# An attention and experts kernel: three tiles for w1, raw tiles of their own for each kind of weights, eight result tiles

## The chip, the cores and the metric

One core of one Trainium2 chip runs the whole program. Times are device microseconds (us) of one execution. The kernel before took 694.74 us as the median of 3 runs (694.33 to 696.3).

## What is computed

Three stages follow each other: attention by random features, a gated block, and four experts whose outputs are mixed by weights. N = 1152 tokens (batch 2 x 576), D = 512 features, F = 1024. All of it is float32.

```python
q_p, k_p = phi(q * scale), phi(k * scale)     # phi: exp of a projection by omega
x = (q_p @ (k_p^T v)) / (q_p @ sum(k_p))      # heads joined: 1152 x 512
x = ((x @ w1) * (x @ w2)) @ w3 @ w_out        # the gated block
p = domain_probs / (domain_probs.sum(-1, keepdims=True) + 1e-09)
for e in range(4):
    out += p[:, e:e + 1] * (np.maximum(x @ ew1[e], 0.0) @ ew2[e])
```

## The kernel before

**Numbers as pairs.** A float32 operand of a matmul is held as a pair: a rounded high part and the rest (HI, LO). `split` makes one: ScalarE (ACT) writes the high part (L79), VectorE (DVE) subtracts it (L80). Three matmuls then stand for one product (`PASSES`). In the profile, "w1e<-raw" on ACT and "w1e<-raw,w1e" on DVE are the two halves of such a split.

**The stages.** Attention runs in pairs of heads, with parts of the gated block beside it. The product of w3 and w_out is folded into `w3o` (eight tiles of 4 KB in each partition). `gated` (L158) multiplies by w1 and w2, whose pairs lie in the pool `w1` (eight tiles of 4 KB). `expert_input` (L204) multiplies by the folded weights, first for batch 0, then for batch 1, eight groups of 24 matmuls each, and splits the experts' inputs, `x2`.

**The experts** run in eight half experts, two for each of the four. A half loads its weights (`load_w1`, `load_w2`), computes the hidden values (`hidden`, L690 on TensorE, PE) for two halves of the columns, forms sums of them (`sums`, tiles hs and hq), and multiplies by the second weights (`second`, L772, and `tails`, L799). Both products are done by Strassen's scheme with seven products in place of eight, so the weights are needed in sums and differences. `load_w1` loads two raw tiles of 4 KB, splits one (a w1e tile of 8 KB), splits a quarter (w1f, 4 KB), adds and subtracts raw parts in place (`place`, L586 on DVE, four times), splits the other raw tile (a second w1e tile), adds again and splits the first one once more (the third w1e tile). `load_w2` does much the same with two raw tiles and four w2e tiles. A product of `hidden` comes in groups of six matmuls: X1 Y1 X5 Y5 and so on in `ORDER`.

**The results.** `second` collects a token tile of results in an `o` tile. In the first seven halves GpSimd's queue adds it to the output in memory (`add_to`, L724). In the last half the output so far is read back into the nine `o` tiles (`results`, L734 on SyncE's queue, SP), DVE adds the last products (L749), and SP stores them (`store`, L740).

**What sets the order.** Each engine runs its instructions in one fixed order. A scheduler writes these orders when the kernel is built, from the dependences, the order of the code, and the tiles that are free: a pool with `bufs` tiles makes the next `tile()` wait until an earlier one has been read for the last time. Pools are placed in SBUF from its left and its right end like two stacks, so a pool that is opened after another was closed lies over the same bytes, and its tiles wait for the last reader there. On the right end the pools of the experts start where `w1` and `w3o` lay: first the pool of w1e and w1f, then w2e, and further in hid, hs, s and o. The raw tiles are a pool on the left.

```python
raw_p = ctx.enter_context(tc.tile_pool(name="raw", bufs=3, reuse_waits="tile"))
w1e_p, w2_p, hid_p, hs_p, s_p, o_p = right("w1e", 4), right("w2e", 4), right("hid", 1), ...
```

Of the kernel before, what the change touches and what calls it, by code (L numbers as in the profile page):

```python
# [8 lines left out]
F32 = mybir.dt.float32  # L9
# [6 lines left out]

HI, LO = 0, 1
HS_BUFS = 4
O_BUFS = 6
HALVES = 5  # L20


# [22 lines left out]
def attention_moe_kernel(ctx: ExitStack, tc: tile.TileContext, q, k, v, omega, mw1, mw2, mw3, mwo, probs, ew1, ew2, out):  # L45
# [6 lines left out]
    P = 128  # L52
# [82 lines left out]
    w12, hid, wo, w3o, x2, xf = {}, {}, [], [], {}, {}  # L135
# [108 lines left out]
    with ExitStack() as actx:  # L244
# [78 lines left out]
        for j in range(2):  # L323
            s = slice(j * D, (j + 1) * D)
# [27 lines left out]
        class Pair:  # L352
# [81 lines left out]
            def place(self):  # L434
                ps = bank("et")
                for r in range(R):
                    transpose(ps[:, r * P:(r + 1) * P], self.xs[:, r].rearrange("p j d -> p (j d)"))
                x, s = xt[self.b][self.i], MAIN_COLS
                split(x[:, HI, s], x[:, LO, s], ps)
# [100 lines left out]
                    else:  # L540
                        gated(at, 2, int(s[1]), int(s[2]), ("w", "po") * 2)

    raw_p = ctx.enter_context(tc.tile_pool(name="raw", bufs=3, reuse_waits="tile"))
    h_p = mctx.enter_context(tc.tile_pool(name="h", bufs=2 * KF + 2 * KD - XT_BUFS, reuse_waits="tile"))
    a_p = cctx.enter_context(tc.tile_pool(name="a", bufs=1, reuse_waits="tile", side="right"))
    for s in AFTER.split():
# [23 lines left out]
    GH = KE // 4  # L570
# [3 lines left out]
    def right(name, bufs):  # L574
        return ctx.enter_context(tc.tile_pool(name=name, bufs=bufs, side="right", reuse_waits="tile"))

    w1e_p, w2_p, hid_p, hs_p, s_p, o_p = right("w1e", 4), right("w2e", 4), right("hid", 1), right("hs", HS_BUFS), right("s", 2), right("o", O_BUFS)
    hd = hid_p.tile([P, 2 * GH, B, S], F32, name="hd")
    turn = [0]

# [7 lines left out]
    def parts(t, src):  # L588
        split(t[:, HI], t[:, LO], src)
        return t  # L590

    def combine(low, high, x11, x12, x21, x22, first, both):


        t = {}
        a = both(low)
        t["A11"], t["A12"] = a[0], a[1]
        t["A22"] = first(x22)
        place(x22, x21, x22, ALU.add)
        place(x21, x11, x21, ALU.subtract)  # L600
        a = both(high)
        t["S3"], t["S1"] = a[0], a[1]
        place(x11, x22, x11, ALU.subtract)
        place(x12, x12, x11, ALU.subtract)
        a = both(low)
        t["S2"], t["S4"] = a[0], a[1]
        return t

    def raw_half(src):
        r = raw_p.tile([P, 2, 512], F32, tag="raw", name="raw")  # L610
        nc.sync.dma_start(out=r.rearrange("p a (k f) -> p (a k) f", f=src.shape[2]), in_=src)
        return r

    def load_w1(hf):

        r = []
        for m in range(2):
            f0 = m * (EFF // 2) + hf * GH * P
            r.append(raw_half(ew1[e, :, f0:f0 + GH * P].rearrange("(k p) f -> p k f", p=P)))

        def both(src):
            t = parts(w1e_p.tile([P, 2, 2, 512], F32R, tag="w1e", name="w1e"), src)
            return [t[:, :, k].rearrange("p a (k f) -> p a k f", k=2) for k in range(2)]

        def first(src):
            t = parts(w1e_p.tile([P, 2, 512], F32R, tag="w1f", name="w1f", bufs=1), src)
            return t.rearrange("p a (k f) -> p a k f", k=2)

        return combine(r[0], r[1], r[0][:, 0], r[0][:, 1], r[1][:, 0], r[1][:, 1], first, both)

    def load_w2(hf):

        r = []
        for m in range(2):
            f0 = m * (EFF // 2) + hf * GH * P
            r.append(raw_half(ew2[e, f0:f0 + GH * P].rearrange("(g p) d -> p g d", p=P)))
        b = {(m, n): r[m][:, :, n * HD:(n + 1) * HD] for m in range(2) for n in range(2)}

        def both(src):
            return parts(w2_p.tile([P, 2, GH, DM], F32R, tag="w2e", name="w2e"), src)  # L640

        t = {}

        def named(x, one, two):
            t[one], t[two] = x[:, :, :, :HD], x[:, :, :, HD:]

        t["both"] = both(r[0]), both(r[1])
        named(t["both"][0], "B11", "B12")
        named(t["both"][1], "B21", "B22")
        place(b[0, 0], b[0, 1], b[0, 0], ALU.subtract)  # L650
        place(b[0, 1], b[1, 1], b[0, 1], ALU.subtract)
        named(both(r[0]), "T1", "T3")
        place(b[1, 1], b[1, 1], b[0, 0], ALU.subtract)
        place(b[1, 0], b[1, 0], b[1, 1], ALU.subtract)
        named(both(r[1]), "T4", "T2")
        return t
# [153 lines left out]
    for e in range(NE):  # L810
        for hf in range(2):
            fresh, last = e == 0 and hf == 0, e == NE - 1 and hf == 1
            with ExitStack() as order:
                for ins in (*pairs[-1].mark, pairs[-1].loaded):
                    order.enter_context(tc.issue_after(ins))
                w1t = load_w1(hf)
            hidden(w1t, 0)
            t0 = sums(0)
            w2t = load_w2(hf)
            hidden(w1t, 1)  # L820
            second(w2t, t0, 0, fresh, last)
            t1 = sums(1)
            tails(w2t, fresh, last)
            second(w2t, t1, 1, fresh, last)
# [30 lines left out]
```

## Time and profile before

| what | value |
|---|---|
| median of 3 runs | 694.74 us |
| the profiled execution: time, span | 693.17 us, 691.4 us |
| PE busy | 665.8 us, 96% |
| DVE busy | 482.7 us, 70% |
| ACT busy | 402.9 us, 58% |
| POOL busy | 163.8 us, 24% |
| mean granted clock of PE | 0.997 of full speed |

The span is the time from the first instruction to the last one; 1.77 us of the execution lie around it. PE's share is the largest by far, and matmuls overlap a little, so its busy time is no measure of its peak. The attention and the gated block end at about 259 us, `expert_input` at about 310 us; the rest is the experts. "DMA" in a table by stretches is the mean busy share of the 16 DMA engines.

### The profile page before, as it was taken

Reading aid. Unit: us, or ns where it says so; the run is one execution under the profiler, and the core shown is the slowest. Engines: PE = TensorE matmul, PEld = TensorE weight load, DVE = VectorE, ACT = ScalarE, POOL = GpSimd, SP = SyncE. Lnnn points to the kernel's source line nnn. Section 1 sums busy time; section 2 is a strip of 40 time slices with the busy share of each in tenths; the row PEclk is TensorE's granted clock in tenths of the full one; section 3 lists DMA queues with packets and bytes.
Section 4 is the critical chain, followed back from the end, with each engine's and each line's share of the span. In section 5 each row is a group of like instructions: output and inputs, shape, how many; then the busy total and the mean of one; then the engine's idle time right before and its main releaser. Section 6 shows DMA issues by size and latency. Waiting matters only on the chain.

```text
span 691.4 us, 12448 instructions
## 1 busy us (share of the span) xinstructions
PE 665.8 (96%) x4889; PEld 634.7 (92%) x4889; DVE 482.7 (70%) x782; ACT 402.9 (58%) x867; POOL 163.8 (24%) x155
## 2 busy tenths in 40 slices
PE   7898999999999999998999999999999999999997
PEld 6786778899999999998989999999999999999996
DVE  4888646669593222258987869877888688688795
ACT  5895445565452222246866676677676676686640
POOL 2865223259271000000021122230320311202200
PEclk9999999999999999999999999999999999999999
DMA  9764323235330000001143166372660762745715
GB/s 260 262 210 140 94 91 116 77 113 153 123 92 1 1 1 1 1 1 61 62 137 122 17 122 122 44 150 68 122 137 2 138 123 27 140 93 100 146 32 167
DMA packets 47146, 66.91 MB, mean 97 GB/s; under 512 B 7600, under 2 KB 30128, under 8 KB 47088
## 3 DMA queue, kind: packets, MB, share of 16 engines
q1 hardware_dynamic: 37792, 49.05, 22.8%
q0 software_dynamic: 8608, 16.52, 15.9%
q8 instruction: 38, 0.62, 0.4%
q10 hardware_dynamic: 688, 0.56, 0.3%
q14 instruction: 20, 0.16, 0.1%
HBM read 47.24 MB, written 18.87 MB: 96 GB/s over the span
## 4 chain that ended last, share of the span: by engine, by line
PE 73%; DVE 11%; DMA 6%; ACT 5%; issue 3%; POOL 1%; DVEq 0%; ACTq 0%; POOLq 0%; SPq 0%
PE ps_po L185 5%; PE ps_f L690 5%; PE ps_f L772 4%; DMA raw<-in_moe_w_dram 3%; PE ps_w L158 3%; PE ps_w L690 3%; PE ps_f L158 3%; PE ps_po L158 3%; PE ps_x L690 3%; PE ps_et L690 3%; PE ps_kv L690 2%; PE ps_t L690 2%; PE ps_po L690 2%; PE ps_kv L772 2%; PE ps_kv L412 2%
## 5 line engine op out<-in xcount | busy, mean ns | idle before, releaser
L724 POOL DMA_DIRECT2D out_dram<-o x70 | 57.7, 892 | 382.5 <-DVE o L749 206.6
L93 POOL TENSOR_SCALAR f64e<-f 128x512 f32<-128x512 f32 x40 | 66.8, 1673 | 78.1 <-DVE w3f L95 32.2
L80 DVE TENSOR_TENSOR hs<-hd,hs 128x1024 fp32r<-128x1024 f32 x48 | 58.4, 1219 | 3.1 <-ACT hs L79 2.4
L79 ACT ACTIVATE hs<-hd 128x1024 fp32r<-128x1024 f32 x48 | 50.7, 1056 | 7.9 <-DVE hd L586 4.9
L185 PE MATMUL ps_po<-wo,w3T 128*128 128x512 f32 x192 | 48.4, 400 | 3.3 <-DVE w3T L80 2.8
L690 PE MATMUL ps_f<-x,w1e 128*128 128x288 f32 x288 | 48.2, 298 | 3.1 <-DVE w1e L80 3.1
L674 ACT ACTIVATE hd<-hd 128x288 f32<-128x288 f32 x96 | 41.3, 439 | 15.6 <-DVE hd L672 14.9
L586 DVE TENSOR_TENSOR raw<-raw 128x512 f32<-128x512 f32 x64 | 43.9, 686 | 8.4 <-DMA raw<-in_moe_w_dram 8.1
L185 PEld LDWEIGHTS ps_po<-wo,w3T 128*128 128x128 f32 x192 | 34.8, 188 | 12.2 <-DVE w3T L80 3.9
L690 PEld LDWEIGHTS ps_f<-x,w1e 128*128 128x128 f32 x288 | 41.8, 191 | 3.7 <-DVE w1e L80 3.6
L94 DVE SCALAR_TENSOR_TENSOR f64e<-f,f64e 128x512 uint32<-128x512 uint32 x40 | 40.1, 1012 | 6.1 <-POOL f64e L93 5.8
L586 DVE TENSOR_TENSOR hd<-hd 128x512 f32<-128x512 f32 x64 | 43.9, 685 | 0.6
L79 ACT ACTIVATE w2e<-raw 128x1024 fp32r<-128x1024 f32 x32 | 33.5, 1058 | 17.7 <-PE ps_f L772 4.7
L772 PE MATMUL ps_f<-w2e,hs 128*128 128x256 f32 x288 | 42.6, 283 | 1.0 <-ACT o L746 0.6
L80 DVE TENSOR_TENSOR w2e<-raw,w2e 128x1024 fp32r<-128x1024 f32 x32 | 38.9, 1219 | 4.6 <-ACT w2e L79 4.5
L80 DVE TENSOR_TENSOR w1e<-raw,w1e 128x1024 fp32r<-128x1024 f32 x24 | 29.3, 1222 | 17.5 <-ACT w1e L79 17.2
L772 PEld LDWEIGHTS ps_f<-w2e,hs 128*128 128x128 f32 x288 | 38.1, 191 | 1.5 <-ACT o L746 0.8
L158 PE MATMUL ps_w<-xt,w 128*128 128x288 f32 x144 | 34.4, 298 | 0.0
L79 ACT ACTIVATE w1e<-raw 128x1024 fp32r<-128x1024 f32 x24 | 25.4, 1059 | 15.2 <-DMA raw<-in_moe_w_dram 10.3
L158 PE MATMUL ps_po<-xt,w 128*128 128x288 f32 x144 | 33.9, 296 | 0.0
L79 ACT ACTIVATE hid<-a 128x288 fp32r<-128x288 f32 x32 | 13.0, 440 | 30.8 <-DVE a L169 30.8
L80 POOL TENSOR_TENSOR w<-w12f,w 128x512 fp32r<-128x512 f32 x16 | 22.0, 1384 | 15.1 <-ACT w L79 15.0
(263 smaller groups left out, 1777.4 us busy)
## 6 DMA issues: line engine op xcount, KB each, us to landing
f<-in_moe_w_dram SPq DMA_DIRECT2D x32, 512.0 KB, 3.7
raw<-in_moe_w_dram SPq DMA_DIRECT2D x32, 512.0 KB, 5.5
out_dram<-o POOLq DMA_DIRECT2D x56, 256.0 KB, 5.2
f<-in_moe_w_out_dram SPq DMA_DIRECT2D x8, 512.0 KB, 5.1
kr<-in_k_dram SPq DMA_DIRECT2D x8, 256.0 KB, 3.8
vr<-in_v_dram SPq DMA_DIRECT2D x8, 256.0 KB, 5.0
o<-out_dram SPq DMA_DIRECT2D x8, 256.0 KB, 3.6
out_dram<-o SPq DMA_DIRECT2D x8, 256.0 KB, 2.5
```

What stands on the lines that cost most here:

```text
L79: nc.scalar.activation(out=hi, in_=src, func=ACTF.Copy)
L80: (eng or nc.vector).tensor_tensor(out=lo, in0=src, in1=hi.bitcast(F32), op=ALU.subtract)
L93: nc.gpsimd.tensor_scalar(out=e.bitcast(F32), in0=high.bitcast(F32), scalar1=0.0, scalar2=None, op0=ALU.mult)
L94: nc.vector.scalar_tensor_tensor(out=e, in0=low, scalar=29, in1=e, op0=ALU.logical_shift_right, op1=ALU.bitwise_or)
L158: nc.tensor.matmul(out=bs[c][:, :HS], lhsT=w12[w, g][:, x, kk], rhs=xt[b][kk][:, y, c * HS:(c + 1) * HS], start=(kk == 0 and n == 0), stop ...
L185: nc.tensor.matmul(out=po, lhsT=wt[:, a, g * P:(g + 1) * P], rhs=wo[hf * 4 + g][:, c], start=(n == 0), stop=(n == 3 * KF - 1),)
L412: nc.tensor.matmul(out=ps[:, j * D1:(j + 1) * D1], lhsT=e, rhs=a, start=(r == 0), stop=(r == R))
L586: nc.vector.tensor_tensor(out=o, in0=x, in1=y, op=op)
L674: nc.scalar.activation(out=h, in_=src, func=ACTF.Relu)
L690: nc.tensor.matmul(out=ps, lhsT=w1t[a][:, x, kk, g * P:(g + 1) * P], rhs=x2[b, kk][:, y, s], start=(k in "125" and kk == 0 and n == 0), st ...
L724: dma = nc.gpsimd.dma_start(out=out[toks, d], in_=src[rows], **({} if fresh else dict(accum_op=ALU.add))).ins
L772: nc.tensor.matmul(out=ps, lhsT=t[a][:, x, g, j * P:(j + 1) * P], rhs=w2t[b][:, y, g], start=(k in "15" and g == 0 and n == 0), stop=(k in ...
```

## The change

Three numbers of tiles change, and one pool is added. The w1e pool has three tiles in place of four. The raw tiles of the first product stay in the old pool, which has two in place of three; those of the second product get a pool of two, `r2`, on the right behind w2e. The pool `o` has eight tiles in place of six. In bytes for each partition: 8 KB less for w1e, 4 KB less for raw, 8 KB more for r2, 4 KB more for o.

```diff
-O_BUFS = 6
+O_BUFS = 8
...
-    raw_p = ctx.enter_context(tc.tile_pool(name="raw", bufs=3, reuse_waits="tile"))
+    raw_p = ctx.enter_context(tc.tile_pool(name="raw", bufs=2, reuse_waits="tile"))
...
-    w1e_p, w2_p, hid_p, hs_p, s_p, o_p = right("w1e", 4), right("w2e", 4), right("hid", 1), right("hs", HS_BUFS), right("s", 2), right("o", O_BUFS)
+    w1e_p, w2_p, r2_p = right("w1e", 3), right("w2e", 4), right("r2", 2)
+    hid_p, hs_p, s_p, o_p = right("hid", 1), right("hs", HS_BUFS), right("s", 2), right("o", O_BUFS)
...
-    def raw_half(src):
-        r = raw_p.tile([P, 2, 512], F32, tag="raw", name="raw")
+    def raw_half(pool, src):
+        r = pool.tile([P, 2, 512], F32, tag="raw", name="raw")
...
-            r.append(raw_half(ew1[e, :, f0:f0 + GH * P].rearrange("(k p) f -> p k f", p=P)))
+            r.append(raw_half(raw_p, ew1[e, :, f0:f0 + GH * P].rearrange("(k p) f -> p k f", p=P)))
...
-            r.append(raw_half(ew2[e, f0:f0 + GH * P].rearrange("(g p) d -> p g d", p=P)))
+            r.append(raw_half(r2_p, ew2[e, f0:f0 + GH * P].rearrange("(g p) d -> p g d", p=P)))
```

PE's order is the same up to the end of `expert_input`. Three places of the new order follow; lines from L587 on are one number higher than before.

DVE, from the last results of the gated block on (x with a number is an input of the experts, b and t with a number are results of `expert_input` for batch 1). Before, the first w1e split stands behind nearly all of `expert_input`:

```order
L225 TENSOR_TENSOR t_3429<-b_3458,ps_w 128x288
L226 TENSOR_TENSOR t_3428<-b_3458,t_3428 128x288
L80 TENSOR_TENSOR w1e<-raw,w1e 128x1024
L80 TENSOR_TENSOR w1f<-raw,w1f 128x512
L80 TENSOR_TENSOR x_3291<-b_3458,x_3291 128x288
L80 TENSOR_TENSOR x_3289<-t_3429,x_3289 128x288
L80 TENSOR_TENSOR x_3288<-t_3428,x_3288 128x288
L586 TENSOR_TENSOR raw<-raw 128x512
```

DVE now, where the gated block ends (a and hid are its values):

```order
L169 TENSOR_TENSOR a<-ps_w,a 128x288
L169 TENSOR_TENSOR a<-ps_po,a 128x288
L80 TENSOR_TENSOR w1e<-raw,w1e 128x1024
L80 TENSOR_TENSOR w1f<-raw,w1f 128x512
L80 TENSOR_TENSOR hid<-a,hid 128x288 x2
L587 TENSOR_TENSOR raw<-raw 128x512
L80 TENSOR_TENSOR x_2982<-xf,x_2982 128x288
L587 TENSOR_TENSOR raw<-raw 128x512 x3
L80 TENSOR_TENSOR w1e<-raw,w1e 128x1024
L80 TENSOR_TENSOR x_3012<-xf,x_3012 128x288
L80 TENSOR_TENSOR w1e<-raw,w1e 128x1024
```

All splits of the first half's w1 have moved from the end of `expert_input` to its beginning; the last two hid splits stand behind the first two of them.

ACT, around the results of the tails in a later half expert (p with a number and hd are values of `hidden`, o are results). Before:

```order
L746 ACTIVATE o<-ps_w,pr 128x256
L678 ACTIVATE p_6810<-ps_po 128x288
L678 ACTIVATE p_6818<-ps_t 128x288
L79 ACTIVATE w1e<-raw 128x1024
L674 ACTIVATE hd<-hd 128x288
L678 ACTIVATE p_6802<-ps_kv 128x288
L746 ACTIVATE o<-ps_et,pr 128x256
L746 ACTIVATE o<-ps_f,pr 128x256
```

ACT now, at the same place:

```order
L747 ACTIVATE o<-ps_w,pr 128x256
L679 ACTIVATE p_6813<-ps_po 128x288
L679 ACTIVATE p_6821<-ps_t 128x288
L679 ACTIVATE p_6805<-ps_kv 128x288
L675 ACTIVATE hd<-hd 128x288
L747 ACTIVATE o<-ps_et,pr 128x256
L747 ACTIVATE o<-ps_f,pr 128x256
```

The w1e conversion, the first one of the half expert after the next, no longer stands between the evictions; it now comes behind the splits of hs, after PE's last use of the tile that it writes.

SP, the last half expert: loads of the output into o and stores. Before:

```order
L734 DMA o<-out_dram 128x512 x4
L734 DMA o<-out_dram 64x512 x2
L734 DMA o<-out_dram 128x512
L740 DMA out_dram<-o 128x512
L734 DMA o<-out_dram 128x512
L740 DMA out_dram<-o 128x512 x3
L734 DMA o<-out_dram 128x512 x2
L740 DMA out_dram<-o 64x512 x2
```

SP now:

```order
L735 DMA o<-out_dram 128x512 x4
L735 DMA o<-out_dram 64x512 x2
L735 DMA o<-out_dram 128x512 x3
L741 DMA out_dram<-o 128x512
L735 DMA o<-out_dram 128x512
L741 DMA out_dram<-o 128x512 x3
L741 DMA out_dram<-o 64x512 x2
```

Eight of the nine tiles are now loaded ahead of the first store, and one behind it (a tile of 64 + 64 rows takes two transfers).

## Rows read from the trace of the kernel before

**Rows 1.** The page, busy times of the engines (share of the span) xinstructions.

```profile
PE 665.8 (96%) x4889; PEld 634.7 (92%) x4889; DVE 482.7 (70%) x782; ACT 402.9 (58%) x867; POOL 163.8 (24%) x155
```

**Rows 2.** By stretches: length, PE PEld DVE ACT POOL busy, PEclk, DMA, GB/s.

```profile
313.00:316.60 3.60, 3.60 (x19) 3.60 (x19) 2.77 (x8) 1.20 (x4) 0.00 (x0) 0.60 0.00 0
...
337.10:360.00 22.90, 21.75 (x154) 19.99 (x155) 20.34 (x29) 16.00 (x29) 2.45 (x5) 1.00 0.28 90
...
360.00:671.00 311.00, 307.58 (x2365) 302.62 (x2364) 248.54 (x362) 214.42 (x415) 55.24 (x66) 1.00 0.49 95
...
671.00:691.40 20.40, 15.73 (x113) 14.35 (x112) 12.13 (x22) 1.58 (x2) 0.00 (x0) 1.00 0.47 155
```

**Rows 3.** Timeline of PE, 306 to 338 us: start, us [idle before <-releaser].

```profile
306.50 3.32 PE L204 MATMUL ps_po<-hid,w3o 128*128 128x288 f32 x24
...
312.52 1.81 PE L690 MATMUL ps_f<-x,w1e 128*128 128x288 f32 x6 [2.71 <-DVE w1e L80]
...
314.13 1.65 PE L690 MATMUL ps_kv<-x,w1e 128*128 128x288 f32 x6
...
323.34 0.96 PE L690 MATMUL ps_kv<-x,w1e 128*128 128x288 f32 x6
...
332.89 0.96 PE L690 MATMUL ps_kv<-x,w1f 128*128 128x288 f32 x6
...
336.05 0.95 PE L690 MATMUL ps_kv<-x,w1e 128*128 128x288 f32 x6
...
337.07 0.98 PE L772 MATMUL ps_x<-w2e,hs 128*128 128x256 f32 x6
```

**Rows 4.** Timeline of ACT and DVE at 310 us: the first w1e conversion.

```profile
310.16 1.05 ACT L79 ACTIVATE w1e<-raw 128x1024 fp32r<-128x1024 f32 x1
...
311.24 1.23 DVE L80 TENSOR_TENSOR w1e<-raw,w1e 128x1024 fp32r<-128x1024 f32 x1
```

**Rows 5.** Timeline of ACT and PE in three later half experts.

```profile
502.61 1.06 ACT L79 ACTIVATE w1e<-raw 128x1024 fp32r<-128x1024 f32 x1 [2.06 <-DMA raw<-in_moe_w_dram]
...
504.71 0.98 PE L772 MATMUL ps_f<-w2e,hs 128*128 128x256 f32 x6 [0.55 <-ACT o L746]
...
551.02 0.98 PE L772 MATMUL ps_w<-w2e,hs 128*128 128x256 f32 x6 [0.31 <-ACT o L746]
...
595.89 1.06 ACT L79 ACTIVATE w1e<-raw 128x1024 fp32r<-128x1024 f32 x1 [1.71 <-DMA raw<-in_moe_w_dram]
...
597.99 0.98 PE L772 MATMUL ps_et<-w2e,hs 128*128 128x256 f32 x6 [0.97 <-ACT o L746]
```

**Rows 6.** Timeline of DVE and PE in the second half expert.

```profile
385.97 1.23 DVE L80 TENSOR_TENSOR hs<-hd,hs 128x1024 fp32r<-128x1024 f32 x1 [0.53 <-ACT hs L79]
...
387.86 0.87 PE L772 MATMUL ps_kv<-w2e,hs 128*128 128x256 f32 x6
...
388.57 0.88 PE L772 MATMUL ps_et<-w2e,hs 128*128 128x256 f32 x6
```

**Rows 7.** Instructions on the raw tiles: duration ns min/median/max.

```profile
L79 ACT ACTIVATE w1e<-raw x24: 1041/1060/1087, 310.2 to 633.0; 128x1024 fp32r<-128x1024 f32 x24
...
L80 DVE TENSOR_TENSOR w1e<-raw,w1e x24: 1216/1222/1227, 311.2 to 634.1; 128x1024 fp32r<-128x1024 f32 x24
...
L586 DVE TENSOR_TENSOR raw<-raw x64: 678/685/695, 314.1 to 650.2; 128x512 f32<-128x512 f32 x64
...
DMA to landing us min/median/max: 3.3/5.5/8.5
```

**Rows 8.** Timeline of DVE and PE in the last half expert.

```profile
677.12 0.48 DVE L749 SCALAR_TENSOR_TENSOR o<-ps_po,pr,o 128x256 f32<-128x256 f32 x1 [1.25 <-DMA o<-out_dram]
...
681.43 0.48 DVE L749 SCALAR_TENSOR_TENSOR o<-ps_w,pr,o 128x256 f32<-128x256 f32 x1 [2.70 <-DMA o<-out_dram]
...
681.97 0.98 PE L772 MATMUL ps_w<-w2e,hs 128*128 128x256 f32 x6 [0.88 <-DVE o L749]
...
687.74 0.48 DVE L749 SCALAR_TENSOR_TENSOR o<-ps_w,pr,o 128x256 f32<-128x256 f32 x1 [0.23 <-PE ps_w L772]
```

## Prediction

> **What bounds the kernel now.** I read the page's busy shares first. TensorE (PE) is busy for 665.8 of 691.4 us [rows 1], so the change can win only where PE stands still or runs at a low clock; work taken from another engine counts only through such a place. Next the table by stages, PE's busy time against a stage's length [rows 2]. From 360 us to 671 us PE is idle for 311.00 - 307.58 = 3.42 us in all, from 337.1 to 360 for 22.90 - 21.75 = 1.15 us. From 313.0 to 316.6 its granted clock is 0.60, so for part of that stretch it was at the lower of its two levels (1.2 in place of 2.4 GHz). In the last 20.40 us it works 15.73 us. The stage that matters is the entry into the experts, 309.8 to 337.1 us.
>
> PE's own timeline shows what ends the wait there [rows 3]. The last matmul of L204 ends at 306.50 + 3.32 = 309.82; the first matmul of an expert starts at 312.52, after 2.71 us for the VectorE (DVE) split of w1e. The next group of six starts 1.61 us after it; later ones take (336.05 - 323.34) / 16 = 0.794 us. The first product of w2e starts at 337.07. Twenty-six groups stand between 309.82 and that start, 20.65 us at full pace, so it could have come at 330.47: **6.6 us are lost at the entry**. The cause stands on ScalarE (ACT) and DVE [rows 4]: the first conversion of expert weights starts at 310.16, after PE's last read of the folded weights, and its second half ends at 311.24 + 1.23 = 312.47. The data had been in SBUF long before; it was the tile's place that was not free.
>
> **The change, part by part.**
>
> *Three w1e tiles.* Three of 8 KB and w1f of 4 KB are 28 KB, which fit into the 32 KB of the first block's weights, read last just ahead of L204. With four, 36 KB, one lies over folded weights that PE reads until 309.82. The new order puts all four w1 splits of the first half expert (three w1e, one w1f) and their four additions at the beginning of `expert_input`, among the splits of the first batch's inputs. That moves 3 x 1.06 us on ACT and 3 x 1.22 + 4 x 0.685 us on DVE [rows 7], with w1f some 7 us of DVE, to where PE runs the sixteen groups of L204 (3.3 us each [rows 3]) without needing them. I cost it at nothing: the last hid splits, which queue behind the first two conversions, are read only by the second batch, eight groups or 25 us later. Without that cover it would be the 1.06 + 1.22 us of one conversion.
>
> The first matmuls of the experts then follow L204 at once, at full clock. What is late next is the second weights. Their raw tiles now lie over the folded weights and over scratch of that stage, so both loads wait for its end, where before one of the two lay in SBUF long ahead. I put the issue at 312.5, the end of the old first conversion [rows 4]: the splits of inputs that it waits for move up into that slot. The load lands after 3.3 to 8.5 us, median 5.5 [rows 7]; the two loads here have the queue to themselves, so I take the low end, 316. The first product of w2e now has 25 groups ahead of it, not 26, and is due at 309.82 + 25 x 0.794 = 329.7. It also needs hs. Before, it came 337.07 - 332.89 = 4.2 us after the start of the last group of the first column half. Now that group, the eighteenth, starts at 309.82 + 17 x 0.794 = 323.3, and two additions and one w2e split have moved into the chain behind it: 2 x 0.685 + 1.22 = 2.6 us. 323.3 + 4.2 + 2.6 = 330.1, 0.4 us late. **Entry: 6.6 - 0.4 = 6.2 us gained**; at most 6.6, plus the 1.15 us after it [rows 2], which I leave standing; at least 1.8, the first rival.
>
> *Own raw tiles.* With three shared, the first conversion for the half after next sits on ACT in front of evictions, and waits for its load: 2.06 and 1.71 us. PE then waits for those evictions: 0.55, 0.31 and 0.97 us [rows 5]. With two raw tiles for each kind, the w1 pair is reloaded as soon as this half's third conversion is done, almost a half expert ahead, and the new order has no w1 conversion between these evictions. Gain 1.83 us; at most the whole 3.42 of the stage.
>
> What it costs: with three w1e tiles the next half's first conversion must wait for PE's last use of the tile, and now stands earlier, beside the splits of hs. Behind it on DVE is the third hs split. In the second half expert that split ended at 385.97 + 1.23 = 387.20, its reader began at 387.86, and DVE had idled 0.53 us ahead of it [rows 6]. A conversion of 1.22 us uses up 0.66 + 0.53, so it costs between 0.03 us and, if the idle time can't be used, 1.22 - 0.66 = 0.56 us; at seven boundaries 0.2 to 3.9 us. I take 0.1 each, 0.7 us, nearer the row that shows the idle time. Steady halves: 1.83 - 0.7 = **1.1 us gained** (from 2.1 lost to 3.4 gained).
>
> The Trainium skill ("Perfetto Trace Analysis", Optimization Strategy) says that the same gap repeating on the engine that should be saturated can mean that there are too few buffers for the next tile. The rule speaks against giving up a w1e tile; the third rival below is what it would do. By the trace, PE's gaps in the steady halves are 3.42 us in all and those shown come from evictions, so I go by the rows.
>
> *Eight result tiles.* The last half reads back nine tiles of the output. With six, the seventh to ninth wait for stores; the last two loads end a DVE wait of 2.70 us at 681.43 and PE waits 0.88 us [rows 8]. With eight, only the ninth waits for a store, the first one; in this trace the reload behind the first store was there at 677.12. Two reloads less on the chain: of PE's 20.40 - 15.73 = 4.67 idle us there [rows 2], 691.40 - 687.74 = 3.66 lie behind the last matmul, which the last update follows, and 1.0 before. **Tail: 1.0 us**, bounds 0.3 (another wait in its place) and 1.0. In the other halves the two tiles only free ACT earlier; PE's waits there are already counted.
>
> **Sum.** 6.2 + 1.1 + 1.0 = 8.3 us. The profiled execution took 693.17 us, so it would take 684.9; the median of the runs is 694.74, 1.57 above it, so I say **686.4 us**.
>
> **Rivals.**
>
> *The second weights become the bound at the entry.* For it: both loads now start only at 312.5, and DVE has three w2e splits ahead of hs. If the load takes the longest time shown, 8.5 us, it lands at 321.0, ACT is done at 322.1, and DVE still has four splits of 1.22, six additions of 0.685 and five smaller ones (at most as long) ahead of PE: 12.4 us, 334.5, against the 329.7 that PE could reach. Entry gain 6.6 - 4.8 = 1.8, in all 3.9: 690.8 us. Against it: the DMA queues are empty there (DMA 0.00 from 313.0 to 316.6, [rows 2]). Chance 0.13.
>
> *The earlier conversion sits in the hs chain for its whole length.* 7 x 1.22 = 8.5 us eat the other gains, 6.2 + 1.83 + 1.0 = 9.0: 694.2 us, no change. Against it: the slack in rows 6. Chance 0.04.
>
> *Slower: the third w1e tile becomes a wait at every boundary.* PE frees the tile, ACT (1.06) and DVE (1.22) convert, PE waits for both: 7 x 2.28 = 16.0 us, less 9.0: 701.7 us. It decides from 9.0 + 2.1 = 11.1 us, 1.6 us a boundary. The rule of the Trainium skill that is cited above speaks for this rival. Against it: between the freeing use and the first need of the new tile the order has 6 groups of the first product (0.794 us [rows 3]) and 14 of the second (388.57 - 387.86 = 0.71 us [rows 6]), 14.7 us against 2.28. Chance 0.04.
>
> *The change doesn't do what it says*, that is, the scheduler leaves the w1 splits late: ruled out by the new order itself, so no chance of its own.
>
> **The numbers.** The forecast has 0.79, the first rival 0.13, the other two 0.04 each. The range begins where nearly all idle time shown is recovered (6.6 + 1.15 + 3.42 + 1.0 = 12.2 us: 682.6; I say 683.0) and ends at the first rival's 690.8. A measurement of this kernel can tell about 0.3% (2.1 us) from no change: faster 0.92, the same 0.04, slower 0.04.
>
> **What would show it.** Right: the first expert matmul within 0.3 us of L204's end, clock 1.00 through 309 to 320 us, the first w2e product near 330 us instead of 337.07, no ACT wait on a raw load after 360 us, no DVE wait for the o loads but perhaps the ninth. Wrong: PE waiting for w2e or hs by more than 1 us near 330 us (first rival), or repeated PE waits for w1e or hs in the steady halves (the other two). If PE's total idle time in 360 to 671 us grows beyond 3.42 us, the steady term has the wrong sign.

## The result and the profile after

The changed kernel takes **685.54 us** (median of 4 runs, 684.64 to 688.66) against 694.8 us before: ratio 0.9871, 95% interval 0.9837 to 0.9906, so it is faster by 0.9 to 1.6%. The forecast was 686.4 us, in a range of 683.0 to 690.8.

The page of its profiled execution (685.55 us, span 683.8 us), busy times as in [rows 1]:

```profile
span 683.8 us, 12451 instructions
...
PE 662.5 (97%) x4889; PEld 633.0 (93%) x4889; DVE 482.6 (71%) x782; ACT 402.8 (59%) x867; POOL 163.6 (24%) x155
```

Each of these engines runs as many instructions as before; DVE, ACT and POOL are busy for the same time within 0.2 us. PE is busy for 3.3 us less, 2.5 of them at the entry (40.67 us in the stretch from the end of L204 to the first tails before, 38.14 now). The table by stretches, in the columns of [rows 2]: behind L204's end, the whole entry, the steady halves.

```profile
311.80:315.40 3.60, 3.60 (x29) 3.60 (x29) 2.42 (x6) 2.92 (x9) 0.00 (x0) 1.00 0.10 16
...
311.80:351.70 39.90, 38.14 (x288) 36.86 (x287) 35.58 (x56) 30.47 (x60) 2.42 (x4) 1.00 0.24 78
...
351.70:671.00 319.30, 316.94 (x2432) 311.81 (x2433) 257.21 (x375) 218.18 (x421) 55.42 (x66) 1.00 0.48 99
```

The granted clock is 1.00 behind L204, where it was 0.60, and PE's idle time in the steady halves is 2.36 us; before, 3.42 in a somewhat shorter stretch.

PE's timeline at the entry into the experts, which answers to [rows 3] (start, us, [idle before <-releaser]):

```profile
308.48 3.32 PE L204 MATMUL ps_po<-hid,w3o 128*128 128x288 f32 x24
311.64 0.96 PE L691 MATMUL ps_f<-x,w1e 128*128 128x288 f32 x6
312.44 0.96 PE L691 MATMUL ps_kv<-x,w1e 128*128 128x288 f32 x6
...
331.53 0.87 PE L773 MATMUL ps_x<-w2e,hs 128*128 128x256 f32 x6
...
335.46 0.95 PE L773 MATMUL ps_po<-w2e,hs 128*128 128x256 f32 x6 [0.76 <-DVE hs L80]
...
337.46 0.97 PE L773 MATMUL ps_po<-w2e,hs 128*128 128x256 f32 x6 [0.26 <-ACT o L747]
338.71 0.98 PE L773 MATMUL ps_t<-w2e,hs 128*128 128x256 f32 x6 [0.27 <-ACT hd L675]
```

The experts now follow L204 without a pause, and the first product of w2e starts 331.53 - 311.80 = 19.73 us behind its end; before it was 27.25.

For a common measure, take the start of the tails (L799, now L800). In every kernel of this study but one (the 719.6 us run below) PE's order has the same number of matmuls between the same points: 186 of `hidden` and 102 of `second` from L204 to the first tails, 2094 from there to the seventh tails. These are their groups by tile, first and last start; the first row holds the first and the last half expert, the second one the seventh. Before:

```profile
L799 PE MATMUL ps_f<-w2e,ht x24: 389/389/497, 355.9 to 678.5; 128*128 128x512 f32 x24
...
L799 PE MATMUL ps_po<-w2e,ht x12: 389/389/397, 633.0 to 635.6; 128*128 128x512 f32 x12
```

After:

```profile
L800 PE MATMUL ps_f<-w2e,ht x24: 387/391/497, 351.7 to 673.1; 128*128 128x512 f32 x24
...
L800 PE MATMUL ps_po<-w2e,ht x12: 387/391/397, 626.9 to 629.4; 128*128 128x512 f32 x12
```

With the end of L204 and the end of PE's last matmul (before 687.70, after 680.07) that gives three parts (starts to the hundredth from PE's timelines). Both kernels were profiled once more later, and stand beside it:

| us | before | before, again | after | after, again |
|---|---|---|---|---|
| end of L204 | 309.82 | 314.56 | 311.80 | 313.35 |
| entry: to the first tails | 46.09 | 45.20 | 39.95 | 39.95 |
| steady: to the seventh tails | 277.13 | 276.64 | 275.10 | 275.12 |
| tail: to the last matmul | 54.66 | 54.16 | 53.22 | 53.21 |
| the three together | 377.88 | 376.00 | 368.27 | 368.28 |

The experts take 9.6 us less by the first profiles, 7.7 us less by the later ones. The two first executions differ by 693.17 - 685.55 = 7.62 us all the same, since in the changed one L204 ended 1.98 us later, with the same order on PE up to there. The second execution of the kernel before (below) shows that this is scatter.

### The profile page after: what moved, and what is told of

Same layout as the page of the kernel before. It is cut to its first block, busy times and chain, and to the rows that moved or that the text cites. A ratio compares the mean times of both kernels' runs of the same rounds, so it can differ in the third digit from the quotient of the medians.

```text
span 683.8 us, 12451 instructions
## 1 busy us (share of the span) xinstructions
PE 662.5 (97%) x4889; PEld 633.0 (93%) x4889; DVE 482.6 (71%) x782; ACT 402.8 (59%) x867; POOL 163.6 (24%) x155
## 4 chain that ended last, share of the span: by engine, by line
PE 82%; DVE 8%; DMA 4%; ACT 3%; issue 2%; POOL 1%; SPq 1%; DVEq 0%; ACTq 0%; POOLq 0%
PE ps_f L691 6%; PE ps_f L773 6%; PE ps_po L185 6%; PE ps_et L691 3%; PE ps_w L691 3%; PE ps_x L691 3%; PE ps_et L773 3%; PE ps_w L158 3%; PE ps_kv L773 3%; PE ps_f L158 3%; PE ps_po L158 3%; PE ps_t L691 3%; PE ps_kv L691 3%; PE ps_po L773 3%; PE ps_po L691 3%; PE ps_t L773 3%
## 5 line engine op out<-in xcount | busy, mean ns | idle before, releaser
L185 PE MATMUL ps_po<-wo,w3T 128*128 128x512 f32 x192 | 48.5, 401 | 3.4 <-DVE w3T L80 2.9
L79 ACT ACTIVATE w2e<-raw 128x1024 fp32r<-128x1024 f32 x32 | 33.2, 1055 | 26.5 <-PE ps_f L773 6.5
L94 DVE SCALAR_TENSOR_TENSOR f64e<-f,f64e 128x512 uint32<-128x512 uint32 x40 | 40.2, 1013 | 7.0 <-POOL f64e L93 6.8
L587 DVE TENSOR_TENSOR raw<-raw 128x512 f32<-128x512 f32 x64 | 43.9, 686 | 0.6
L587 DVE TENSOR_TENSOR hd<-hd 128x512 f32<-128x512 f32 x64 | 43.8, 685 | 0.6 <-ACT hd L675 0.2
```

The lines of the kernel that those rows point to most:

```text
L79: nc.scalar.activation(out=hi, in_=src, func=ACTF.Copy)
L94: nc.vector.scalar_tensor_tensor(out=e, in0=low, scalar=29, in1=e, op0=ALU.logical_shift_right, op1=ALU.bitwise_or)
L185: nc.tensor.matmul(out=po, lhsT=wt[:, a, g * P:(g + 1) * P], rhs=wo[hf * 4 + g][:, c], start=(n == 0), stop=(n == 3 * KF - 1),)
L587: nc.vector.tensor_tensor(out=o, in0=x, in1=y, op=op)
```

## Experiments

**Three w1e tiles alone.**

```diff
-    w1e_p, w2_p, hid_p, hs_p, s_p, o_p = right("w1e", 4), right("w2e", 4), right("hid", 1), right("hs", HS_BUFS), right("s", 2), right("o", O_BUFS)
+    w1e_p, w2_p, hid_p, hs_p, s_p, o_p = right("w1e", 3), right("w2e", 4), right("hid", 1), right("hs", HS_BUFS), right("s", 2), right("o", O_BUFS)
```

> The kernel before with three w1e tiles in place of four, and nothing else of the change. Theory (the place of the tiles): with 28 KB the w1e pool lies wholly over the first block's weights, so the first expert matmul starts within 0.3 us of the end of L204 and the first w2e product some 20 us behind that end, where it was 27.25 us before. This alone gives 5.5 to 6.7 us: 688.1 to 689.3 us. ACT still waits 1.5 to 2 us for raw loads in two later half experts. Rival (the raw tiles make the gain, through earlier loads): at most 2 us, 692.8 or more. On the stages ahead: the profiled execution of the changed kernel had the end of L204 1.98 us later than the kernel before, with the same order on TensorE. If that is a cost of the two raw tiles (the tiles behind them move), the end stands near 309.8 us here; if it is scatter between executions, it may stand anywhere from 309.8 to 311.8.

687.23 us (6 runs, 685.78 to 688.36); ratio to before 0.9888 (0.986 to 0.9915). The first expert matmul follows at once, the first w2e product stands 21.20 us behind L204. Entry 40.2 us, steady 275.1, tail 54.4, together 369.75: 8.1 of the 9.6 us. L204 ends at 312.24. The time is below the range expected; the miss is the wait for raw loads, which did not stay. ACT's waits for transfers from 340 us on, in the kernel before:

```profile
ACT w1e L79 <- DMA raw<-in_moe_w_dram: 10.0, 5, 2.2
...
ACT o L746 <- DMA out_dram<-o: 3.1, 3, 1.6
```

(us in all, times, longest) and with three w1e tiles, still three shared raw tiles:

```profile
ACT o L746 <- DMA out_dram<-o: 2.2, 2, 1.4
```

No wait for a raw load is left, and with them go PE's waits for evictions of [rows 5]. In the order of this run the first conversion for the next half stands later, behind PE's last use of the tile, and by then the load has landed.

**The change without raw tiles of its own.** Three shared ones, as before.

```diff
-    raw_p = ctx.enter_context(tc.tile_pool(name="raw", bufs=2, reuse_waits="tile"))
+    raw_p = ctx.enter_context(tc.tile_pool(name="raw", bufs=3, reuse_waits="tile"))
...
-    w1e_p, w2_p, r2_p = right("w1e", 3), right("w2e", 4), right("r2", 2)
+    w1e_p, w2_p = right("w1e", 3), right("w2e", 4)
...
-            r.append(raw_half(r2_p, ew2[e, f0:f0 + GH * P].rearrange("(g p) d -> p g d", p=P)))
+            r.append(raw_half(raw_p, ew2[e, f0:f0 + GH * P].rearrange("(g p) d -> p g d", p=P)))
```

> The changed kernel without raw tiles of its own for each kind: three shared ones, as before; three w1e and eight result tiles stay. Theory: entry and tail as in the changed kernel, ACT waits for raw loads in the steady halves again; 1.1 us slower than the changed kernel, 686.6 us (bounds 683.4 to 688.9). Rival (raw tiles make most of the gain): 690 us or more. End of L204: near 309.8 us if two raw tiles cost time in the stages ahead, anywhere from 309.8 to 311.8 if that was scatter.

687.02 us (684.38 to 688.36), ratio 0.9881 (0.9849 to 0.9913). Experts 368.56 us against 368.27: raw tiles of their own are worth 0.3 us in place of the 1.1 expected, all at the entry (40.2 against 39.95); steady 275.1 in both. The medians differ by 1.5 us, but that is not the experts: the profiled execution ended L204 at 313.01.

**Same tiles, another place.** The raw tiles of the second product stand first on the right, so the w1e pool moves along and lies over folded weights again.

```diff
-    w1e_p, w2_p, r2_p = right("w1e", 3), right("w2e", 4), right("r2", 2)
+    r2_p, w1e_p, w2_p = right("r2", 2), right("w1e", 3), right("w2e", 4)
```

> The changed kernel with the same sizes and numbers of tiles, but the two raw tiles of the second product placed first on the right end, so that the w1e pool moves 8 KB along and one of its tiles lies over folded weights again, as in the kernel before. Theory (it is the place, not the number): the first expert matmul waits some 2.7 us behind L204 for the w1e split, the granted clock falls after it, the first w2e product stands some 27 us behind L204; 6.2 us slower than the changed kernel, 691.7 us. Rival (three tiles in place of four matter by themselves, or the raw tiles make the gain): as the changed kernel, 685.5 us within 1 us.

695.41 us (12 runs, 691.15 to 697.3 and one of 1302.44), ratio to before 1.0003 (0.9982 to 1.0024): the gain is gone. PE's timeline:

```profile
310.28 3.32 PE L204 MATMUL ps_po<-hid,w3o 128*128 128x288 f32 x24
...
316.31 1.06 PE L691 MATMUL ps_f<-x,w1e 128*128 128x288 f32 x6 [2.71 <-DVE w1e L80]
...
323.03 1.06 PE L691 MATMUL ps_et<-x,w1e 128*128 128x288 f32 x6 [1.67 <-DVE w1e L80]
...
327.04 1.07 PE L691 MATMUL ps_f<-x,w1e 128*128 128x288 f32 x6 [2.15 <-DVE w1e L80]
```

The wait is back to the hundredth, with two more behind it. Entry 48.5 us, 8.5 longer than in the changed kernel; steady 275.1, tail 53.2, as there. So the place of the pool sets the entry, and the rival (numbers, not place) falls. That it lost 8.5 and not 6.2 us is nearly all the second and third wait, 3.8 us together; before, waits of this kind were 1.12 and 0.41. The clock did not fall behind the first wait, as expected, but behind the third, for 3.4 us, so this entry holds a loss to the clock as that of the kernel before does:

```profile
328.60:332.00 3.40, 3.40 (x17) 3.40 (x16) 2.03 (x3) 2.17 (x5) 0.00 (x0) 0.50 0.56 144
```

**Six result tiles.** `O_BUFS = 6`, the rest as changed.

> The changed kernel with six result tiles in place of eight. Theory: in the last half expert the seventh to ninth tile wait for stores again, DVE waits 1 to 3 us for o loads; 1.0 us slower than the changed kernel, 686.5 us (0.3 to 1.0 slower). Rival: another wait stands in its place in the last half, no difference within 0.3 us, 685.5 us.

687.1 us (686.64 to 688.11), ratio 0.9887 (0.9861 to 0.9913). DVE's waits in the last half expert:

```profile
DVE o L750 <- DMA o<-out_dram: 3.3, 2, 2.4
```

In the changed kernel there is none of this kind. Tail 54.1 against 53.2 us, the experts 369.11 against 368.27: 0.8 us. With shared raw tiles (the first two runs) the two more result tiles give 1.2 us.

**Four w1e tiles, the fourth elsewhere.** The kernel before with its own numbers and sizes; only every fourth w1e tile comes from a place behind the other pools, so that the tile over folded weights is first used by the next half.

```diff
-    w1e_p, w2_p, hid_p, hs_p, s_p, o_p = right("w1e", 4), right("w2e", 4), right("hid", 1), right("hs", HS_BUFS), right("s", 2), right("o", O_BUFS)
+    w1e_p, w2_p, hid_p, hs_p, s_p, o_p = right("w1e", 3), right("w2e", 4), right("hid", 1), right("hs", HS_BUFS), right("s", 2), right("o", O_BUFS)
+    w1g_p = right("w1g", 1)
...
+    count = [0]
...
-            t = parts(w1e_p.tile([P, 2, 2, 512], F32R, tag="w1e", name="w1e"), src)
+            count[0] += 1
+            pool = w1g_p if count[0] % 4 == 0 else w1e_p
+            t = parts(pool.tile([P, 2, 2, 512], F32R, tag="w1e", name="w1e"), src)
```

> The kernel before with the same number and sizes of tiles, but with the fourth w1e tile in a pool of its own behind the others, so that the tile over the folded weights is first used by the next half expert. Theory (place alone makes the entry, the number of tiles makes the steady halves): the tails of the first half expert start 40.3 us behind the end of L204, as with three tiles (40.26), where before it was 46.1; the fifth to seventh half experts keep the evictions behind a w1e conversion that waits for its load, and last 46.3 to 46.7 us from tails to tails, as before, against 45.5 to 46.1 with three tiles. In all 6 us faster than before, 688.3 us, and 1 to 2 us slower than the run with three tiles alone. Rival (the number of tiles makes both): no gain at the entry, 694 us. Second rival (place makes both): as with three tiles alone, 687.2 us, halves of 45.5 to 46.1 us.

685.69 us (683.16 to 687.45), ratio 0.9864 (0.9834 to 0.9895): 2.6 us better than expected. Entry 38.2 us, 7.9 shorter than before, 2.0 shorter than with three tiles alone and 1.7 than in the changed kernel; tail 54.1. So the place alone makes the entry, and giving up the fourth tile takes part of it back. DVE in the changed kernel puts a w1e split, the next half's first one, and a w2e split between two hs splits:

```profile
329.37 1.21 DVE L80 TENSOR_TENSOR hs<-hd,hs 128x1024 fp32r<-128x1024 f32 x1
...
330.87 1.21 DVE L80 TENSOR_TENSOR w1e<-raw,w1e 128x1024 fp32r<-128x1024 f32 x1
...
332.37 1.21 DVE L80 TENSOR_TENSOR w2e<-raw,w2e 128x1024 fp32r<-128x1024 f32 x1
...
334.10 1.22 DVE L80 TENSOR_TENSOR hs<-hd,hs 128x1024 fp32r<-128x1024 f32 x1
```

With four tiles neither stands there:

```profile
327.32 1.23 DVE L80 TENSOR_TENSOR hs<-hd,hs 128x1024 fp32r<-128x1024 f32 x1
...
330.39 1.22 DVE L80 TENSOR_TENSOR hs<-hd,hs 128x1024 fp32r<-128x1024 f32 x1
```

4.73 us from one hs split to the next against 3.07, and PE's wait of 0.76 us for hs is gone (one of 1.06 us for hd stands ahead of it). The steady part took 275.3 us, which would speak for the second rival; ACT waited 11.0 us for raw loads all the same. The repetition below decides.

**Raw tiles between the w1e and the w2e pool.**

```diff
-    w1e_p, w2_p, r2_p = right("w1e", 3), right("w2e", 4), right("r2", 2)
+    w1e_p, r2_p, w2_p = right("w1e", 3), right("r2", 2), right("w2e", 4)
```

> The changed kernel with the raw tiles of the second product between the w1e and the w2e pool, so that one of them lies over the first block's weights and is loaded early; the w1e pool stays where it is. Theory: the entry stays (first expert matmul at once behind L204), and the second weights are no longer late: the tails of the first half expert start 39.0 to 39.9 us behind L204's end (39.95 in the changed kernel, where TensorE waited 0.76 us for hs): 0 to 1 us faster, 684.5 to 685.5 us. Rival (the second weights were not what was late): no difference, 685.5 us.

685.61 us (684.61 to 686.35), ratio 0.9865 (0.9834 to 0.9896). Experts 367.92 us, entry 39.6, 0.3 us shorter, which lies in the range of the theory. The wait for hs went, one of 1.5 us for hd came. The medians show no difference, as the rival has it; so 0.3 us is all that this place of the second raw tiles was worth.

**Three shared raw tiles, nine result tiles.** As the second run, with `O_BUFS = 9`.

> Three w1e tiles, three shared raw tiles as before, nine result tiles. Theory: raw tiles of their own are worth 0.3 us only (the run with three shared raw tiles took 368.56 us from the end of L204 to the last matmul, the changed kernel 368.27), and the ninth tile frees the last half expert of its last wait for a store; TensorE had none there with eight. So as the run with three shared raw tiles, 687 us, experts 368.2 to 368.6 us. Rival (the ninth load matters): 0.3 to 1 us less.

685.56 us (685.12 to 687.71), ratio 0.9869 (0.984 to 0.9898). Experts 368.54 us against 368.56 with eight: the ninth tile brings nothing. The median is that of the changed kernel, though no kind of weights has raw tiles of its own here.

**The kernel before, once more.**

> The kernel before, profiled once more. The end of L204 stood at 309.82 us in its first profile, and at 311.80 to 313.60 us in the five others, of which all have changed tiles. If that is scatter between executions (the granted clock falls for a while ahead of 80 us in some), it may stand anywhere from 309.8 to 313.6 us here; if the changes cost it, within 0.3 us of 309.8 again. From there to the last matmul it should take 377.9 us again, within 0.5 us.

L204 ended at 314.56 us, later than in any other profile up to then; so the 1.98 us of the changed kernel's first profile are scatter, and not its cost. The experts took 376.0 us, not 377.9. The granted clock explains a part of both. Stretches, first of this execution, around 50 us and behind PE's wait at the entry (columns as in [rows 2]):

```profile
50.00:60.00 10.00, 8.05 (x47) 6.83 (x45) 8.00 (x13) 6.94 (x20) 8.22 (x6) 0.83 0.65 206
...
314.50:317.20 2.70, 0.06 (x1) 0.00 (x0) 2.08 (x5) 2.60 (x6) 0.00 (x0) 1.00 0.00 0
317.20:320.80 3.60, 3.53 (x26) 3.54 (x27) 3.60 (x10) 1.82 (x5) 0.00 (x0) 1.00 0.01 2
```

And of the first execution of the same kernel:

```profile
50.00:60.00 10.00, 8.38 (x48) 6.62 (x48) 9.11 (x14) 8.96 (x26) 7.89 (x6) 1.00 0.65 194
...
309.80:312.50 2.70, 0.02 (x1) 0.00 (x0) 2.08 (x4) 2.65 (x6) 0.00 (x0) 0.99 0.00 0
312.50:316.10 3.60, 3.58 (x15) 3.58 (x16) 3.25 (x7) 0.93 (x3) 0.00 (x0) 0.53 0.01 2
```

After the same idle time of 2.7 us, PE's granted clock was 1.00 in the one and 0.53 in the other, close to the lower of its two levels (1.2 of 2.4 GHz) (26 and 15 matmuls in 3.6 us). Over the whole entry:

```profile
309.80:355.90 46.10, 40.67 (x289) 38.68 (x288) 42.17 (x64) 34.16 (x65) 2.40 (x4) 0.96 0.21 65
```

```profile
314.60:359.80 45.20, 39.20 (x289) 37.24 (x289) 42.14 (x64) 34.43 (x65) 2.40 (x4) 1.00 0.21 66
```

40.67 - 39.20 = 1.5 us of PE's busy time were the clock's.

Ahead of the experts, some 2 of the 4.7 us by which L204 ended later are no matter of the clock, which was 1.00 from 8 to 20 us: PE waited there for a load of q, which the first execution did not do.

```profile
17.07 0.63 PE L109 MATMUL ps_t<-ident,tail 128*128 128x128 f32 x4 [2.20 <-DMA tail<-in_q_dram]
```

**Four w1e tiles with raw tiles of their own.** The changed kernel with the fourth w1e tile of the run above, and four result tiles, which is what fits.

```diff
-O_BUFS = 8
+O_BUFS = 4
...
+    w1g_p = right("w1g", 1)
...
+            count[0] += 1
+            pool = w1g_p if count[0] % 4 == 0 else w1e_p
```

> Four w1e tiles, the fourth in a pool of its own behind the others as in the run with the same sizes as before, raw tiles of their own for each kind of weights, and four result tiles (what fits). It tests the step of the prediction that raw tiles of their own take ACT's waits for raw loads away. Theory (either of the two takes them away, so that with three w1e tiles the raw tiles of their own had nothing left to do): ACT waits for raw loads 0 to 1 us in all after 340 us, where the run with four tiles and three shared raw tiles had 11.0 us in 6 waits; the fifth to seventh half experts last 45.5 to 46.0 us. With four result tiles the last half and the evictions wait more for stores, 0 to 3 us. In all 684 to 688 us. Rival (only the number of w1e tiles takes them away): ACT waits for raw loads 8 us or more again.

719.6 us (711.9 to 723.39), ratio 1.0318 (1.026 to 1.0375): the theory falls, and the rival holds with more than it asked for. The profiled execution took 723.39 us, the longest of the six. ACT's waits from 340 us on, in the same columns as above:

```profile
ACT w1e L79 <- DMA raw<-in_moe_w_dram: 26.5, 5, 6.5
...
ACT o L751 <- DMA out_dram<-o: 7.5, 6, 2.1
```

One of the five, on the timelines of ACT and PE:

```profile
502.85 1.07 ACT L79 ACTIVATE w1e<-raw 128x1024 fp32r<-128x1024 f32 x1
...
510.70 1.06 ACT L79 ACTIVATE w1e<-raw 128x1024 fp32r<-128x1024 f32 x1 [6.48 <-DMA raw<-in_moe_w_dram]
...
513.33 1.81 PE L695 MATMUL ps_t<-x,w1e 128*128 128x288 f32 x6 [5.15 <-ACT o L751]
```

The first row is this half's third conversion, the second one the next half's first. With two raw tiles the reload can only start when the third conversion is done; with a free w1e tile the scheduler puts the next conversion right behind it, so ACT stands still while it loads, and evictions queue behind. PE waits 2.3 to 5.2 us for an eviction five times, and its granted clock is 0.96 from 360 to 635 us, where the last run below has 1.00, so a part of the loss is the clock's.

**The changed kernel and the four-tile one, once more, on one chip.**

> The changed kernel once more, beside the run that follows. From the end of L204 to the last matmul it should take 368.3 us again, within 0.3 us, since no wait there depends on the granted clock's scatter; the end of L204 anywhere from 309.8 to 314.6 us. Median 685.5 us, within 1 us.

685.74 us (685.22 to 688.37), ratio 0.9868 (0.9828 to 0.9908); experts 368.28 us against 368.27 at first.

> The kernel before with only the place of the fourth w1e tile changed, once more, against the changed kernel on the same chip. Its experts took 367.55 us from the end of L204 to the last matmul, the changed kernel's 368.27: 0.7 us faster, median 685 us. Rival: its first profile was a lucky one, and it is 1 to 2 us slower than the changed kernel, as its steady halves with waits for raw loads would have it.

686.01 us (685.06 to 687.82), ratio 0.9869 (0.9829 to 0.9909); experts 370.67 us, where the first profile had 367.55: the steady part took 278.1 us, 2.9 more. ACT's waits for raw loads were 13.7 us, the longest 4.5:

```profile
ACT w1e L79 <- DMA raw<-in_moe_w_dram: 13.7, 6, 4.5
```

The rival was right that the first profile was a lucky one. Its 1 to 2 us show in these profiles (2.4 us) but not in the medians, 686.01 and 685.74, by which the two kernels can't be told apart; so no version here beats the changed kernel.

**Four w1e tiles, shared raw tiles, four result tiles.** It takes the two edits of the 719.6 us run apart; against the run with four w1e tiles above:

```diff
-O_BUFS = 6
+O_BUFS = 4
```

> Four w1e tiles, the fourth placed behind the others, three shared raw tiles, four result tiles: the run with four w1e tiles and raw tiles of their own, without the raw tiles of their own. That run took 719.6 us with 26.5 us of ACT waits for raw loads, and had two edits against the one with four w1e tiles, shared raw tiles and six result tiles (685.7 and 686.0 us). Theory (raw tiles of their own next to four w1e tiles cost it: the next half's first conversion is then put right behind this half's third one, whose raw tile it must reload): 687 to 691 us here, ACT waits for raw loads 11 to 15 us. Rival (the four result tiles cost it): 710 us or more, the waits for raw loads as in that run.

690.87 us (687.68 to 696.91), ratio 0.9947 (0.9908 to 0.9985). So the fewer result tiles cost some 5 us, nearly all in the last half (tail 59.9 us against 54.1), and raw tiles of their own beside four w1e tiles the other 719.6 - 690.87 = 28.7 us (by two chips' medians). The waits for raw loads were 2.7 us, not 11 to 15, and the steady part took 274.6 us: the order had moved again, and with the conversions at these places four tiles cost nothing there.

## Why the prediction was right, and where not

**Entry, 6.2 us forecast: 46.09 - 39.95 = 6.1 measured**, 5.25 against the second profile of before. The mechanism held step by step: place, no wait, clock 1.00, first w2e product 19.73 us behind L204 (PE's own pace gave 19.85). The run with the same tiles in another place shows the cause. Two details differ. The 0.4 us late for hs came as 0.76 us, and at PE's next hs, not at the first. And part of the 6.6 us lost before hung on the clock, 1.5 us of it, which the second execution did not lose; its second w1e wait was 1.68 us in place of 1.12. That the term meets the first profile so closely is in part luck.

**Steady halves, 1.1 us forecast: 2.0 measured** (1.5 between the later profiles). The step that failed is the cause: "With two raw tiles for each kind, the w1 pair is reloaded as soon as this half's third conversion is done ... and the new order has no w1 conversion between these evictions." I read the new order of the whole change and gave its merit to the raw tiles, so the sign was right for another reason than the one given. Three w1e tiles alone give 275.1 us, and raw tiles of their own add nothing there; beside four w1e and four result tiles they cost 28.7 us. In all eight profiles with three w1e tiles ACT waits for no raw load after 340 us, and the steady part takes 275.1 us; in all six with four it waits, for 2.7 to 26.5 us. The fourth tile let the order put ACT's conversion ahead of its load; what that cost differed from kernel to kernel and between two executions of one (steady part 274.6 to 278.1 us with shared raw tiles, 275.3 and 278.1 in the same kernel).

The sum counted PE's idle time alone. PE from the first to the seventh tails, before and after:

```profile
355.91:633.04 277.13, 273.70 (x2094) 268.75 (x2095) 221.40 (x318) 191.93 (x371) 49.38 (x60) 1.00 0.48 96
...
351.75:626.85 275.10, 272.82 (x2094) 268.44 (x2095) 220.68 (x318) 191.80 (x372) 50.24 (x60) 1.00 0.48 97
```

The idle time falls by 1.15 us (3.43 to 2.28), the size forecast but from other terms: the waits of [rows 5] are gone (1.83 us), and one of 0.5 us for hd; two waits for w1e are new. The busy time of the same matmuls falls by 0.88 us. Groups of six start 0.79 us apart in a row but last 0.96 us [rows 3], so a stop takes an overlap away besides the idle time shown. That would explain the rest; no run shows it alone.

The cost term, 0.7 us for the earlier conversion in the hs chain, was too small and mostly in the wrong place. In that chain it shows, together with a w2e split, at the first boundary, where the entry is 1.7 to 2.0 us longer than with four tiles (above). In the steady part of the changed kernel PE waits for w1e itself:

```profile
447.30 1.06 PE L691 MATMUL ps_t<-x,w1e 128*128 128x288 f32 x6 [0.70 <-DVE w1e L80]
...
493.36 1.06 PE L691 MATMUL ps_x<-x,w1e 128*128 128x288 f32 x6 [0.72 <-DVE w1e L80]
```

That is 1.4 us at two of seven boundaries: the third rival's mechanism, with 1.4 of its 16.0 us. The Trainium skill ("Perfetto Trace Analysis", Optimization Strategy) takes a repeating gap on the engine that should be busy as a possible sign of too few buffers. The trace agrees for these two gaps: none of the six profiles with four w1e tiles has a wait of PE for w1e in the steady part. But the one buffer more brought ACT's waits for loads, and no net gain.

**Tail, 1.0 us forecast: 1.4 measured**, 1.0 between the later profiles. Alone, the two more tiles gave 0.8 and 1.2 us. As forecast, DVE no longer waits for an o load.

**Sum.** 8.3 us forecast; 9.6 and 7.7 in the experts by the two pairs of profiles, 694.8 - 685.54 = 9.3 by the medians. The first rival (second weights late by 4.8 us) did not come: PE never waited for w2e at the entry.

## What to carry to other kernels

Where a pool is laid over bytes of an earlier stage, the stage's last reader releases it: a tile count that seems generous can push the first tile of the next stage over weights still in use, and moving one tile elsewhere helps as much as giving one up. One buffer more is not always better: it lets a fixed order place work ahead of its load, in front of work that is ready. When several numbers change at once, run each alone before crediting one, and compare stages between two events of the same trace, where whole times scatter by more than the effect. A stage that waits for loads scatters by itself (367.55 and 370.67 us in two profiles of one kernel), so it needs more than one profile.

## What the runs showed that I had not expected

The same kernel with the same waits does not always get the same clock: after 2.71 us of idle time PE's granted clock fell to 0.53 in one of two executions of the kernel before, and stayed at 1.00 in the other. In the run with another place it stayed at 1.00 behind that wait and fell to 0.50 behind a later one of 2.15 us. Early in the program, from 50 to 60 us, it was 0.83 in some executions and 1.00 in others; the end of L204 stood anywhere from 309.82 to 314.56 us, not by the clock alone: in the first profile of the changed kernel it came 1.98 us late, with 1.00 from 50 to 60 us too. From there on, with no wait on loads, two executions agreed within 0.01 us.
